# Attention with a feed-forward network: nine feed-forward passes of 512 tokens, fp32 scores for the first eight units, key sums over 1728 columns, and a fixed program order

## The chip, the cores and the metric

The kernel runs on one core of one Trainium2 chip. The metric is the device time of one execution in microseconds (us). Before the change three runs took 1312.46, 1313.7 and 1315.76 us; their median is 1313.7 us.

## The reference

Attention over 8 batches and 8 heads, 1152 keys and head size 64. Each two neighbouring queries are averaged first, so there are 576 query rows per head. The output of all heads, laid out as 4608 tokens of 512 numbers, goes through a feed-forward network with three input matrices and a maximum over their products.

```python
q_pool = q.reshape(B, H, S // factor, factor, D).mean(axis=3)
scores = scale * np.matmul(q_pool, k.transpose(0, 1, 3, 2))
scores = scores - np.max(scores, axis=-1, keepdims=True)
attn = np.exp(scores)
attn = attn / (np.sum(attn, axis=-1, keepdims=True) + 1e-09)
return np.matmul(attn, v).astype(np.float32)
...
h = np.maximum(np.maximum(x @ w1, x @ w2), x @ w3)
return (h @ w_out).astype(np.float32)
```

## The kernel before

**Units.** Two heads make a pair (32 pairs, four to a batch), and half of a pair's queries (288) make a unit `d` (64 units, eight to a batch). A unit holds all 1152 keys in nine steps of 128 keys on the partitions, with 2 x 288 columns for the two heads. Per step the TensorE makes the scores `pqk` (L596, L597), ACT copies them to `s` (L609) and DVE keeps a running maximum `acc` over the steps (L618). Then the maximum over the partitions is taken, DVE subtracts it (L743; for the second head of units 0 to 7 POOL does), ACT takes the exponential (L749), the TensorE multiplies with the values into `pav` (L790), and POOL adds the nine steps into `ksum` (L766, L768) for the denominator. In units 0 to 15 the TensorE adds all or part of the steps instead (`psum`, L874).

**Precision.** The scores and the feed-forward use the fp32r type, with every operand split into a high part and the rest. For keys and queries ACT casts the high part (L474, L481), POOL subtracts (L478, L485), and DMAs on the SP queue (`move_k`, `move_q`, L519) stack high and low parts on the 128 partitions in `kc` and `qq`; a score step is then two matmuls of 288 columns per head. `pav` and `psum` are plain fp32, and the two heads go to different columns of the array (`o.pav[64 * h : 64 * h + 64]`).

**Feed-forward.** Batch `b` is one pass of 576 tokens in two chunks of 288. A chunk of 128 hidden numbers is 12 matmuls (`ph`, L1127: four input slices times the products high-high, low-high, high-low); ACT copies the first of three products to `hm` (L1145), DVE takes the maximum with the other two (L1147), ACT and POOL split the result into `h` (L1155, L1158). The second layer is 18 matmuls per chunk and output slice (`po`, L1181), copied out by ACT (L1197) and stored. The weights, split once in pass 0, are read again in every later pass from `w_split` into a ring of two tiles. Pass `b` is put into the program beside the attention of batch `b + 1`; the last pass follows the attention.

**Order.** Every instruction belongs to a step with the steps it needs. `arrange` plays the program with costs (`pe`, `act`, `dve`, `pool`) and takes on each engine the ready step of lowest rank, from the numbers in `RANK` and `TUNE`. The order is fixed when the program is built; each engine then works its own list in order.

## Time and profile before

| | |
|---|---|
| median of three runs | 1313.7 us |
| span of the profiled execution | 1315.8 us |
| time of the profiled execution beside its span | 1315.8 us: the span is as long as the slowest of the three times (1315.76), so nothing lies around it |
| PE, POOL, DVE, ACT busy | 98%, 81%, 76%, 74% of the span |
| unit 8's first score copy | about 136 us |
| last score copy of unit 63 | 1193.3 us |
| read from and written to HBM | 158.47 MB, 22.02 MB |

A busy share says how much of the span has at least one instruction of the engine in it. Matmuls overlap in the records (one of 288 columns is shown with 296 ns, while they start some 132 ns apart), so what a matmul costs is read from how many start in a stretch, not from its length. Idle time stands behind the bar of a group, with the engine that ended it.

### The profile page before, as it was taken

To read this page: it belongs to the slowest core of one execution; us is meant where nothing else is said; L and a number is where in the kernel's file an instruction comes from. 1 tells how busy PE (TensorE), PEld (TensorE's weight loads), DVE (VectorE), ACT (ScalarE), POOL (GpSimd) and SP (SyncE) were. 2 spreads that over 40 slices of the span, in tenths; PEclk is the share of its full clock that TensorE was granted. 3 is DMA by queue.
4 is the path that set the end of the run, shared out by engine and by line. 5 is a ranking of instruction groups with operands and counts; after the bars stand their busy time and mean duration, and the time that the engine had idled before them with its cause. 6 is when DMAs were issued, how large, how long until landed. Compare 5 with 4: busy or idle time off the path is not lost.

```text
span 1315.8 us, 26773 instructions
## 1 busy us (share of the span) xinstructions
PE 1288.9 (98%) x9726; PEld 1112.9 (85%) x9726; DVE 998.9 (76%) x1602; ACT 972.7 (74%) x1863; POOL 1068.1 (81%) x894
## 2 busy tenths in 40 slices
PE   7899999999999999999999999999999999999999
PEld 6555788778888899888889988888899888888998
DVE  5687788988778878888888887888888877885120
ACT  6798788888777877778877887778777777775211
POOL 5678597989999998899988898999988999878210
PEclk7999999999999999999999999999999999999999
DMA  6766477877765676676766577666776567632544
GB/s 185 208 185 159 128 226 234 245 230 215 228 193 178 203 241 205 169 211 184 224 207 205 170 220 223 179 179 197 203 237 195 178 186 213 208 127 81 188 160 157
DMA packets 107795, 255.39 MB, mean 194 GB/s; under 512 B 14608, under 2 KB 78608, under 8 KB 98448
## 3 DMA queue, kind: packets, MB, share of 16 engines
q1 hardware_dynamic: 107376, 253.09, 63.8%
q8 instruction: 78, 1.28, 0.4%
q10 hardware_dynamic: 288, 0.59, 0.1%
q14 instruction: 53, 0.43, 0.1%
HBM read 158.47 MB, written 22.02 MB: 137 GB/s over the span
## 4 chain that ended last, share of the span: by engine, by line
PE 81%; DMA 7%; ACT 5%; POOL 3%; DVE 2%; issue 1%; SPq 1%; ACTq 0%; DVEq 0%; POOLq 0%
PE ph L1127 31%; PE pav L790 20%; PE pqk L596 10%; PE pqk L597 9%; PE po L1181 8%; DMA w<-w_split 3%; PE psum L874 2%; ACT s L609 2%; DMA qq<-qraw 2%; ACT s L749 1%; DMA kraw<-in_kT_dram 1%; DVE acc L618 1%; POOL ksum L768 1%; SPq L519 1%; DMA w<-in_win_dram 1%
## 5 line engine op out<-in xcount | busy, mean ns | idle before, releaser
L768 POOL TENSOR_TENSOR ksum<-ksum,s 128x576 f32<-128x576 f32 x360 | 517.9, 1442 | 9.9 <-ACT s L749 0.4
L1127 PE MATMUL ph<-xh,w 128*128 128x288 f32 x2304 | 511.7, 296 | 3.5 <-DMA w<-w_split 2.2
L609 ACT COPY s<-pqk 128x576 f32<-128x576 f32 x576 | 365.1, 639 | 103.7 <-PE pqk L597 97.5
L618 DVE TENSOR_TENSOR acc<-acc,pqk 128x576 f32<-128x576 f32 x448 | 333.7, 745 | 109.9 <-ACT s L609 106.1
L749 ACT ACTIVATE s<-s 128x864 f32<-128x864 f32 x384 | 351.6, 931 | 61.1 <-DVE s L743 58.1
L1127 PEld LDWEIGHTS ph<-xh,w 128*128 128x128 f32 x2304 | 387.7, 188 | 5.4 <-ACT hm L1145 2.2
L596 PE MATMUL pqk<-qq,kc 128*128 128x288 f32 x1152 | 336.1, 308 | 15.4 <-DVE acc L618 10.4
L1127 PE MATMUL ph<-xl,w 128*128 128x288 f32 x1152 | 339.5, 295 | 0.0
L597 PE MATMUL pqk<-qq,kc 128*128 128x288 f32 x1152 | 324.3, 298 | 0.0
L790 PE MATMUL pav<-s,v 128*64 128x288 f32 x2304 | 291.5, 408 | 0.0
L596 PEld LDWEIGHTS pqk<-qq,kc 128*128 128x128 f32 x1152 | 220.1, 191 | 56.7 <-DVE acc L618 20.5
L790 PEld LDWEIGHTS pav<-s,v 128*64 128x64 f32 x2304 | 160.5, 137 | 113.3 <-issue 9.1
L743 DVE TENSOR_TENSOR s<-s,spare 128x864 f32<-128x864 f32 x216 | 219.9, 1041 | 1.2
L597 PEld LDWEIGHTS pqk<-qq,kc 128*128 128x128 f32 x1152 | 220.8, 192 | 0.0
L1127 PEld LDWEIGHTS ph<-xl,w 128*128 128x128 f32 x1152 | 217.3, 189 | 0.0
L1181 PE MATMUL po<-h,w 128*128 128x288 f32 x1152 | 170.4, 295 | 2.3 <-ACT ob L1197 2.1
L1181 PEld LDWEIGHTS po<-h,w 128*128 128x128 f32 x1152 | 158.5, 188 | 3.9 <-ACT ob L1197 3.3
L743 DVE TENSOR_TENSOR s<-s,pmb 128x864 f32<-128x864 f32 x144 | 148.2, 1043 | 0.8
L1147 DVE TENSOR_TENSOR hm<-hm,ph 128x288 f32<-128x288 f32 x192 | 85.0, 443 | 71.5 <-PE ph L1127 71.0
L1158 POOL TENSOR_TENSOR h<-hm,h 128x288 fp32r<-128x288 f32 x96 | 76.9, 811 | 76.3 <-ACT h L1155 75.8
L766 POOL TENSOR_TENSOR ksum<-s 128x576 f32<-128x576 f32 x56 | 81.8, 1461 | 25.6 <-ACT s L749 25.0
L485 POOL TENSOR_TENSOR kraw<-kraw 128x1152 fp32r<-128x1152 f32 x31 | 83.2, 2684 | 19.3 <-ACT kraw L481 18.9
(62 smaller groups left out, 1035.0 us busy)
## 6 DMA issues: line engine op xcount, KB each, us to landing
w<-w_split SPq DMA_DIRECT2D x63, 1024.0 KB, 6.0
kc<-kraw SPq DMA_DIRECT2D x372, 96.0 KB, 3.5
qq<-qraw SPq DMA_DIRECT2D x248, 144.0 KB, 4.1
w<-w_split SPq DMA_DIRECT2D x28, 768.0 KB, 4.6
v<-in_vr_dram SPq DMA_DIRECT2D x32, 576.0 KB, 4.4
kraw<-in_kT_dram SPq DMA_DIRECT2D x31, 576.0 KB, 4.4
qraw<-in_qT_dram SPq DMA_DIRECT2D x31, 576.0 KB, 5.3
w<-in_win_dram SPq DMA_DIRECT2D x18, 512.0 KB, 4.8
```

The costliest lines, as they stand in the source:

```text
L485: vec[e].tensor_tensor(lo.bitcast(F32R), lo, o.hl[:, 0, x:y], op=ALU.subtract)
L596: nc.tensor.matmul(ps[:, h - hs[0], :QH], w, qq[:, 0, h], start=True, stop=False)
L597: nc.tensor.matmul(ps[:, h - hs[0], :QH], w, qq[:, 1, h], start=False, stop=True)
L609: nc.scalar.copy(o.s[kk // 3][:, kk % 3, slice(*hs)], o.ps[kk, hs][:, :, :QH])
L618: nc.vector.tensor_tensor(acc, acc, ps, op=ALU.max)
L743: vec[e].tensor_tensor(s, s, o.pb[h][:, None, :QH].broadcast_to([P, 3, QH]), op=ALU.subtract)
L749: nc.scalar.activation(s, s, AF.Exp, scale=SCALE)
L768: vec[e].tensor_tensor(o.ksum, o.ksum, x, op=ALU.add)
L790: nc.tensor.matmul(o.pav[64 * h : 64 * h + 64, :QH], pr.v[:, kk, h], o.s[kk // 3][:, kk % 3, h], start=(kk == 0), stop=(kk == NK - 1),)
L1127: nc.tensor.matmul(t.ps[:, :QH], w[:, a, kk], xx[:, kk, qs], start=(kk == 0 and i == 0), stop=(kk == 3 and i == 2),)
L1147: nc.vector.tensor_tensor(part[c], part[c], t.ps[:, :QH], op=ALU.max)
L1181: nc.tensor.matmul(t.ps[:, :QH], w[:, k : k + P], hh[:, kk, qs], start=(kk == 0 and i == 0), stop=(kk == 5 and i == 2),)
```

## The change

Five parts, in one diff.

- The feed-forward runs over `PASSES = [[512]] * 9`: nine passes with one chunk of 512 tokens. Pass boundaries no longer fall on batch boundaries, so a unit's output is split in up to two pieces (`pieces_of`), and the attention output lies in a ring of four halves (`RING`). The weights are fetched eight times instead of seven, into a ring of three tiles (`w3pool`). The second layer waits for each hidden slice alone, not for all.
- In units 0 to 7 (pairs 0 to 3, `WHOLE = 4`) the scores are one plain fp32 matmul per head and step, on the 64 partitions that the head's keys and queries have as loaded: head 0 on rows 0 to 63 of the array, head 1 on rows 64 to 127, each into a bank of its own. The casts, subtractions and stacking DMAs of these pairs go, and so do the inputs `fq` and `fk` laid out for pair 0.
- From unit 16 on POOL makes the key sums as two additions over three steps at once (1728 columns) and two of 576, instead of eight of 576.
- The order is a table, `ORDER`: one place for each step, in the order in which the code makes the steps. `arrange` sorts by it.
- The five groups of six warming matmuls are put among the first units' scores, where before all stood ahead of them.

```diff
-order = arrange(plan, {"ff": 2})
+ORDER = {
+    "warm": [1, 7, 37, 49, 67],
+    "table": [4],
+    "lead": [0, 6, 2, 3, 5],
...
+WHOLE = 4
+PASSES = [[512]] * 9
+START = [sum(map(sum, PASSES[:p])) for p in range(len(PASSES) + 1)]
+XW = max(map(sum, PASSES))
+RING = 4
...
+def arrange(plan):
+    place = {kind: iter(at) for kind, at in ORDER.items()}
+    for s in plan:
+        s.place = next(place[s.kind])
+    assert all(a.place < s.place for s in plan for a in s.after + s.pre)
+    return sorted(plan, key=lambda s: s.place)
...
+def mm(n):
+    return pe(3 * (n / 2.4 + 12.5))
...
                     for h in range(*hs):
-                        w = kc[:, h, kk % 3 * P : kk % 3 * P + P]
+                        if d < 2 * WHOLE:
+                            rows = slice(64 * h, 64 * h + 64)
+                            w, x = pr.k[rows, P * kk : P * kk + P], pr.q[rows, 1, QH * o.half : QH * o.half + QH]
+                            nc.tensor.matmul(ps[:, h - hs[0], :QH], w, x, start=True, stop=True)
+                            continue
+                        w, qq = pr.kc[kk // 3][:, h, kk % 3 * P : kk % 3 * P + P], pr.qq[o.half]
                         nc.tensor.matmul(ps[:, h - hs[0], :QH], w, qq[:, 0, h], start=True, stop=False)
                         nc.tensor.matmul(ps[:, h - hs[0], :QH], w, qq[:, 1, h], start=False, stop=True)
...
+        def thirds(e, i):
+            if i == 1:
+                room()
+                vec[e].tensor_tensor(o.three, o.s[0], o.s[1], op=ALU.add)
+            else:
+                vec[e].tensor_tensor(o.three, o.three, o.s[2], op=ALU.add)
+
+        def fold(e, i):
+            vec[e].tensor_tensor(o.ksum, o.ksum, o.three[:, i], op=ALU.add)
...
+    def pieces_of(b, half):
+        t = NQ * b + QH * half
+        for p, (x, y) in enumerate(zip(START, START[1:])):
+            lo, hi = max(t, x), min(t + QH, y)
+            if lo < hi:
+                yield p, lo - x, hi - lo, lo - t
...
+                wt[g] = (w3pool if place % 3 == 2 else wpool).tile([P, 2, 2, NPAIR, P], F32R, tag="w", name=f"w{b}_{g}")
...
                             for i, (a, xx) in enumerate(((0, xh), (0, xl), (1, xh))):
                                 nc.tensor.matmul(
-                                    t.ps[:, :QH],
+                                    t.ps[:, :n],
                                     w[:, a, kk],
                                     xx[:, kk, qs],
...
-                        "mm", at, n, [pe(396)], product, [tail[0]] + fetched[g] + (hdone if kk == 0 else []),
-                        take="ff" if kk == 0 else None, cols=864,
+                        "mm", at, done * NQ / total, [mm(n)], product, [tail[0]] + fetched[g] + hdone[kk, c],
+                        take="ff" if kk == 0 else None, cols=3 * n,
...
     finish[d - 1]([])
-    ffn(B - 1, [0, 1], d)
-
-    order = arrange(plan, {"ff": 2})
+    for p in range(B - 1, len(PASSES)):
+        ffn(p, d + 8 * (p - B + 1))
+
```

The first place is the ACT list at the program's start, before; names carry the unit (`s0` and `pqk0` are unit 0's), and `qq`, `kc` hold the split queries and keys.

```order
L372 DMA qraw0_0_120<-in_fq_dram 128x576 x2
L411 ACT_TABLE_LOAD
L411 COPY rest_117<-ones_99 128x1
L382 CAST qq0_0_149<-qraw0_0_120 128x288
L403 CAST kc0_0_164<-kraw0_129 128x384
L382 CAST qq0_0_149<-qraw0_0_120 128x288
L403 CAST kc0_0_164<-kraw0_129 128x384
L609 COPY s0_0_184<-pqk0_0_174 128x576
L609 COPY s0_0_184<-pqk0_1_179 128x576
L403 CAST kc0_1_192<-kraw0_129 128x768
L609 COPY s0_0_184<-pqk0_2_187 128x576
L403 CAST kc0_2_204<-kraw0_129 128x768
```

And the same list with the change.

```order
L242 DMA q0_122<-in_qT_dram 128x2x288
L223 ACT_TABLE_LOAD
L223 COPY rest_134<-ones_102 128x1
L460 COPY s0_0_151<-pqk0_0_145 128x576
L460 COPY s0_0_151<-pqk0_1_148 128x576
L460 COPY s0_0_151<-pqk0_2_154 128x576
L460 COPY s0_1_166<-pqk0_3_162 128x576
```

The six casts that stood ahead of and between unit 0's first score copies are gone; ACT's first work on data is the copy of a score step.

The second place is POOL around the key sums of unit 40, before; `xl`, `xr`, `kraw` and `ks` belong to other units and wait in the same list.

```order
L766 TENSOR_TENSOR ksum40_9274<-s40_0_8916 128x576
L949 TENSOR_TENSOR xl_114<-xr_112,xh_113 128x288
L833 TENSOR_TENSOR ks38_8991<-ks38_8991,ky39_64_9302 64x36
L768 TENSOR_TENSOR ksum40_9274<-ksum40_9274,s40_0_8916 128x576
L833 TENSOR_TENSOR ks38_8991<-ks38_8991,ky39_32_9316 32x36
L768 TENSOR_TENSOR ksum40_9274<-ksum40_9274,s40_1_8985 128x576
L949 TENSOR_TENSOR xl_114<-xr_112,xh_113 128x288
L768 TENSOR_TENSOR ksum40_9274<-ksum40_9274,s40_1_8985 128x576
L805 TENSOR_TENSOR xr_112<-xr_112,rs38_9386 128x288
L768 TENSOR_TENSOR ksum40_9274<-ksum40_9274,s40_1_8985 128x576
```

And with the change.

```order
L620 TENSOR_TENSOR ksum40_7613<-s40_0_7252,s40_1_7312 128x1728
L1071 TENSOR_TENSOR h3_6526<-hm3_5_0_7539,h3_6526 128x512
L622 TENSOR_TENSOR ksum40_7613<-ksum40_7613,s40_2_7360 128x1728
L715 TENSOR_TENSOR ks38_7595<-ks38_7595,ky39_64_7684 64x36
L625 TENSOR_TENSOR ksum40_7613<-ksum40_7613 128x576
L320 TENSOR_TENSOR kraw22_7642<-kraw22_7642 128x1152
L625 TENSOR_TENSOR ksum40_7613<-ksum40_7613 128x576
```

Eight additions have become four, and what stands between them (here a feed-forward half and a key preparation) now stands behind an addition of three times the columns.

The third place is PE where the attention ends and the feed-forward of the last tokens begins, before; `pav62` and `pav63` are the last two units' products with the values, `po6` the second layer of pass 6, `ph7` the first layer of pass 7.

```order
L790 MATMUL pav63_14832<-s63_2_14605,v31_14056 64x288 x6
L1181 MATMUL po6_0_0_14855<-h6_13591,w6_9_14722 128x288 x18
L1181 MATMUL po6_0_1_14878<-h6_13591,w6_9_14722 128x288 x18
L1181 MATMUL po6_1_0_14904<-h6_13591,w6_10_14799 128x288 x18
L1181 MATMUL po6_1_1_14935<-h6_13591,w6_10_14799 128x288 x18
L1181 MATMUL po6_2_0_14968<-h6_13591,w6_11_14908 128x288 x18
L1181 MATMUL po6_2_1_14994<-h6_13591,w6_11_14908 128x288 x18
L1181 MATMUL po6_3_0_15016<-h6_13591,w6_12_14963 128x288 x18
L1181 MATMUL po6_3_1_15040<-h6_13591,w6_12_14963 128x288 x18
L1127 MATMUL ph7_0_0_0_15065<-xh_113,w7_0_15020 128x288
```

And with the change.

```order
L1094 MATMUL po6_3_0_12053<-h6_10892,w6_12_11989 128x512 x18
L672 MATMUL pav62_12082<-s62_0_11586,v31_11517 64x288 x6
L672 MATMUL pav62_12082<-s62_1_11648,v31_11517 64x288 x6
L672 MATMUL pav62_12082<-s62_2_11702,v31_11517 64x288 x6
L672 MATMUL pav63_12125<-s63_0_11810,v31_11517 64x288 x6
L672 MATMUL pav63_12125<-s63_1_11846,v31_11517 64x288 x6
L672 MATMUL pav63_12125<-s63_2_11886,v31_11517 64x288 x6
L1029 MATMUL ph7_0_0_0_12163<-xh_115,w7_0_12029 128x512
```

Before, eight chunks of the second layer (18 matmuls of 288 columns each) stand between the last attention product and the first layer of pass 7, the last pass. With the change the whole second layer of pass 6 stands ahead of the last two attention products, pass 7 follows them at once, in matmuls of 512 columns, and pass 8 follows pass 7.

## Rows read from the trace of the kernel before

**Rows 1.** The page: busy time, share of the span and instructions of each engine.

```profile
PE 1288.9 (98%) x9726; PEld 1112.9 (85%) x9726; DVE 998.9 (76%) x1602; ACT 972.7 (74%) x1863; POOL 1068.1 (81%) x894
```

**Rows 2.** The page: the chain that ended last, by engine.

```profile
PE 81%; DMA 7%; ACT 5%; POOL 3%; DVE 2%; issue 1%; SPq 1%; ACTq 0%; DVEq 0%; POOLq 0%
```

**Rows 3.** Windows: start:end length, busy (instructions) by engine, granted clock, DMA.

```profile
0.00:9.00 9.00, 7.26 (x35) 7.09 (x36) 3.68 (x9) 3.17 (x6) 1.58 (x10) 1.00 0.58 199
9.00:136.00 127.00, 114.72 (x785) 71.85 (x784) 91.68 (x154) 102.89 (x179) 91.34 (x62) 0.89 0.65 182
...
283.00:1041.00 758.00, 753.96 (x5753) 669.71 (x5752) 627.65 (x984) 597.19 (x1159) 689.33 (x574) 1.00 0.68 202
...
1193.00:1237.00 44.00, 43.43 (x330) 39.17 (x330) 14.39 (x26) 16.83 (x41) 26.54 (x28) 1.00 0.43 150
1237.00:1316.00 79.00, 75.32 (x565) 74.81 (x564) 10.89 (x24) 13.18 (x32) 9.69 (x12) 1.00 0.44 160
```

**Rows 4.** Windows of the tiles ph and po alone, in the tail.

```profile
1241.00:1279.00 38.00, 37.64 (x284) 37.44 (x283) 6.81 (x15) 3.19 (x8) 1.00 0.46 167
...
1297.00:1310.00 13.00, 13.00 (x99) 12.92 (x98) 2.00 (x5) 1.00 0.54 190
```

**Rows 5.** A window at the half clock, and timeline of PE: start, us, instruction.

```profile
15.00:20.00 5.00, 4.30 (x16) 3.48 (x15) 2.43 (x4) 2.96 (x5) 2.25 (x2) 0.50 0.48 135
...
17.83 0.44 PE L597 MATMUL pqk<-qq,kc 128*128 128x288 f32 x1
18.07 0.44 PE L596 MATMUL pqk<-qq,kc 128*128 128x288 f32 x1
```

**Rows 6.** Timeline of weight loads and matmuls after a short idle.

```profile
8.62 0.19 PEld L596 LDWEIGHTS pqk<-qq,kc 128*128 128x128 f32 x1 [0.18 <-DVE kc L408]
8.72 0.19 PEld L597 LDWEIGHTS pqk<-qq,kc 128*128 128x128 f32 x1
...
8.62 0.40 PE L596 MATMUL pqk<-qq,kc 128*128 128x288 f32 x1
8.85 0.29 PE L597 MATMUL pqk<-qq,kc 128*128 128x288 f32 x1
```

**Rows 7.** Window of the tile pav; timeline of PE from pav to pqk.

```profile
500.00:1000.00 500.00, 116.36 (x936) 66.07 (x936) 10.24 (x26) 1.00 0.67 200
...
723.69 1.62 PE L790 MATMUL pav<-s,v 128*64 128x288 f32 x12
725.25 0.40 PE L596 MATMUL pqk<-qq,kc 128*128 128x288 f32 x1
```

**Rows 8.** Groups by line and form on POOL: count, busy us, mean ns, idle before.

```profile
L768 POOL TENSOR_TENSOR ksum<-ksum,s 128x576 f32<-128x576 f32 x360 | 517.9, 1442 | 9.9 <-ACT s L749 0.4
L485 POOL TENSOR_TENSOR kraw<-kraw 128x1152 fp32r<-128x1152 f32 x31 | 83.2, 2684 | 19.3 <-ACT kraw L481 18.9 <-DMA w<-w_split 0.2
L1158 POOL TENSOR_TENSOR h<-hm,h 128x288 fp32r<-128x288 f32 x96 | 76.9, 811 | 76.3 <-ACT h L1155 75.8
```

**Rows 9.** Groups by line and form on ACT: casts of keys and queries.

```profile
L481 ACT CAST kraw<-kraw 128x1152 fp32r<-128x1152 f32 x31 | 35.9, 1158 | 8.9 <-DMA kraw<-in_kT_dram 4.8 <-DMA qq<-qraw 4.0
L474 ACT CAST qraw<-qraw 128x576 fp32r<-128x576 f32 x31 | 20.9, 676 | 3.8 <-POOL qraw L471 2.7 <-DMA w<-w_split 0.5
```

**Rows 10.** Groups by line and form on DVE: maxima over scores and feed-forward.

```profile
L618 DVE TENSOR_TENSOR acc<-acc,pqk 128x576 f32<-128x576 f32 x448 | 333.7, 745 | 109.9 <-ACT s L609 106.1
L1147 DVE TENSOR_TENSOR hm<-hm,ph 128x288 f32<-128x288 f32 x192 | 85.0, 443 | 71.5 <-PE ph L1127 71.0
```

**Rows 11.** Timeline of ACT and POOL at the end of the attention.

```profile
1193.30 0.64 ACT L609 COPY s<-pqk 128x576 f32<-128x576 f32 x1 [1.08 <-PE pqk L597]
...
1225.49 0.80 POOL L949 TENSOR_TENSOR xl<-xr,xh 128x288 fp32r<-128x288 f32 x1 [0.55 <-ACT xh L946]
```

**Rows 12.** The page: DMA issues, KB each, us to landing; timeline: the last copy.

```profile
w<-w_split SPq DMA_DIRECT2D x63, 1024.0 KB, 6.0
...
1312.76 0.40 ACT L1197 COPY ob<-po 128x288 f32<-128x288 f32 x1 [1.99 <-PE po L1181]
```

More of the change, by code (lines that the diff above doesn't have):

```diff
@@ new lines, in loads @@
+        def loads(fn, parts, size, lead, eng, more):
+            if n:
+                gone = [qk[pairs[n - 2].last, NK - 1]] if n > 1 else pairs[0].kmoved + pairs[0].qmoved
+                return [step("load", r, [("sp", 0.5)], lambda e: fn(e, *parts[0]), gone + more, size=parts[0][1] * size)]
+            return [
+                Step(plan, "lead", [(eng if i == 0 else "sp", 0.4)], lambda e, x=x, y=y: fn(e, x, y), [], size=(y - x) * size)
+                for i, (x, y) in enumerate(parts)
+            ]
@@ new lines, in whole @@
+        o.qmoved = loads(load_q, qparts, 1, -1000, "act", [])
+        o.kmoved = loads(load_k, kparts, 0.5, -1001, "sp", o.qmoved)
+        inline("qq", o.qmoved)
+        inline("ksum", o.kmoved)
+        qs = [
+            step("prep", r + 0.01 * i, [(pool if n else dve)(y - x)], lambda e, x=x, y=y: qsum(e, x, y), [a])
+            for i, ((x, y), a) in enumerate(zip(qparts, o.qmoved))
+        ]
+        o.kready = {c: [o.kmoved[c % len(o.kmoved)]] for c in range(3)}
+        o.qready = {half: [qs[half % len(qs)]] for half in range(2)}
@@ L445, in load_v @@
+        loaded = o.kmoved + o.qmoved
+        if n == 1:
+            pairs[0].lv.after += loaded
+        o.lv = step(
+            "load",
+            r + 2,
+            [("sp", 0)],
+            lambda e: load_v(e, o, n, b, j),
+            [av[pairs[n - 2].last]] if n > 1 else loaded + ([pairs[0].lv] if n else []),
+            size=576,
+        )
+        inline("v", [o.lv])
     def load_v(e, o, n, b, j):
@@ L537, in heads @@
             o.qmoved += o.qready[half]
+            inline("qq", o.qready[half])
             if d == r:
                 for c in range(3):
-                    i = 3 * n + c - 4
-                    gone = qk[pairs[i // 3].last, 3 * (i % 3) + 2] if i >= 0 else None
+                    i = 3 * (n - WHOLE) + c - 4
+                    gone = qk[pairs[WHOLE + i // 3].last, 3 * (i % 3) + 2] if i >= 0 else None
                     o.kready[c] = [
@@ L764, in key @@
                 if kk == 1:
-                    o.ksum = small.tile([P, 2, QH], F32, tag="ksum", name=f"ksum{d}")
+                    room()
                     vec[e].tensor_tensor(o.ksum, o.s[0][:, 0], x, op=ALU.add)
@@ L967, in rest @@
                 for g in range(4):
-                    t = [step("psum", d, [("act", 0.3)], hand(g), t + [gone])]
+                    t = [step("psum", d, [("act", 0.3)], hand(g), t + [gone], pre=[spreads.get(15) if d == 17 else None])]
                 folded[d] = folded[d - 1] = t[0]
@@ L1143, in half @@
+                        if b == f == j == c == kk == 0:
+                            tail[0].pre += held
+                        done += 6 * n / QH / 2
+                    def half(e, t=t, j=j, c=c, f=f, n=n, part=part):
                         if j == 0:
-                            part[c] = small.tile([P, QH], F32, tag="hm", name=f"hm{b}_{f}_{c}", bufs=3)
-                            nc.scalar.copy(part[c], t.ps[:, :QH])
-                        else:
-                            nc.vector.tensor_tensor(part[c], part[c], t.ps[:, :QH], op=ALU.max)
@@ L1149, in ffn @@
-                    used = len(hm_read) + c - cs[0] - 3
+                            part[c] = small.tile([P, 512], F32, tag="hm", name=f"hm{b}_{f}_{c}", bufs=HM)
+                            nc.scalar.copy(part[c][:, :n], t.ps[:, :n])
+                        else:
+                            nc.vector.tensor_tensor(part[c][:, :n], part[c][:, :n], t.ps[:, :n], op=ALU.max)
+                    used = len(hm_read) + c - HM
                     first = [tail[0], prev[c] if j else hm_read[used] if used >= 0 else None]
-                    prev[c] = ffn_step("evac", at, n, [act(QH) if j == 0 else dve(QH)], half, first, give="ff")
+                    prev[c] = ffn_step("evac", at, done * NQ / total, [act(n) if j == 0 else dve(n)], half, first, give="ff")
```

540 lines of the change are left out of this document (191 added, 349 removed), and 6 rows, old and new, of tables (ORDER, TUNE).

## The prediction

> **What bounds the kernel now.** I read the busy shares first, then the chain that ended last, then the same shares stretch by stretch, since an average hides where the limits change. PE is busy for 98% of the span, the next engine (POOL) for 81% [rows 1], and PE holds 81% of the last chain [rows 2]. By stretches there are three regimes [rows 3]. From 9 to 136 us (units 0 to 7, no feed-forward to fill with) no engine is full: PE is busy for 114.7 of 127 us at a mean granted clock of 0.89, ACT for 102.9. From 283 to 1041 us PE is busy for 753.96 of 758 us, with POOL at 689.33, 91%. From 1193 us on PE works almost alone. So outside the first stretch a microsecond taken off PE's own work is a microsecond of the span, as long as POOL, the next, does not take over.
>
> PE's records overlap, so the price of a matmul is a pitch. In the tail 284 first-layer matmuls stand in 38.00 us (133.8 ns each) and 99 of the second layer in 13.00 us (131.3 ns) [rows 4]; I use 132.5 ns for 288 columns.
>
> **The feed-forward at 512 columns.** Before, a pass is 2 x (18 x 12 + 4 x 18) = 576 matmuls, and eight passes are 4608 x 132.5 ns = 610.6 us. After, a pass is 288 matmuls and nine are 2592. What one of 512 columns costs no row shows; the question is what the 132.5 ns are made of, because 288 columns at 2.4 GHz are only 120 ns.
> - At the half clock of 1.2 GHz (0.50 in the window) matmuls start 0.24 us apart [rows 5]: exactly 288 / 1.2 GHz and nothing else. So the 12.5 ns are not added to the columns at that clock; something about 130 ns long runs beside them, and shows only when the columns are shorter.
> - The weight load is such a thing. After a short idle the first load starts at 8.62, the second, which waits for the first to be taken over, at 8.72, and the second matmul at 8.85 [rows 6]: 0.10 for a load, then 0.13 to the next matmul, even with weights and columns free to overlap.
> - In fp32, where a record streams 288 columns in two cycles each (240 ns), 936 records are 116.36 us busy, 26 units of 4.475 us with 18 starts of two records each [rows 7]; less the last one's overhang that is 240 ns and at most a few more per start.
>
> So with 213.3 ns of columns the load should lie under them, and I take 215 ns: 2592 x 215 = 557.3 us, **53.3 us less**. The other ends: 12.5 ns on top of each matmul after all (225.8 ns, 585.3 us, 25.3 us less), or a cost in proportion to the columns (235.6 ns, 610.6 us, nothing less). Nothing below that: no row has a matmul that costs more per column with more columns.
>
> The Trainium skill's page "TensorE: Matmul & The Clock Gate", section "Back-to-back issue gap", gives a lone warm matmul N / 2.4 GHz plus 2.5 ns, 215.8 ns at 512 columns and 122.5 at 288. For 288 the rows have 132.5, so the measurement decides there; with the page's price on both sides the gain would be 4608 x 122.5 - 2592 x 215.8 ns = 5 us, with the measured price before it is 51. The 10 ns that the page does not have are what the first rival keeps.
>
> The copies and maxima of 512 columns replace two of 288: on DVE 443 ns for 288 and 745 for 576 [rows 10] give 0.68 us for 512 against 0.89, less on every engine, hidden as before. Weights: a tile serves 24 matmuls, 5.2 us, and lands in 6.0 [rows 12]; with three tiles its load has two tiles' time, 10.3 us, where it had 6.4. I cost it at nothing; if the cover went, it would be under 1 us per tile.
>
> **Scores of units 0 to 7.** 72 steps of four matmuls (0.53 us) become two fp32 matmuls on half the rows each. The nearest row is the pair in `pav`, on half the columns each: 4.475 / 9 = 0.50 us per pair [rows 7]. Beside each other: 2 us less in all; one after the other (2 x 0.48): 31 us more. I take them as beside each other, like `pav`, and at 0 for the span, since PE does not set the end in this stretch.
>
> The Trainium skill's page "TensorEngine Tiling (Array Packing)", section "Key Properties", speaks against it: a change of tiling mode drains the array. Twelve `pav` records take 1.56 us to the first score (723.69 to 725.25), where six starts at 4.475 / 18 = 0.249 are at most 1.49 [rows 7], so the drain is there and costs some 0.1 us. Some 70 such changes lie ahead of unit 8, about as many as before; were each to drain twice, PE would have 7 us more to do there.
>
> **The start.** Per pair ACT loses casts of 1158 and 676 ns [rows 9], POOL subtractions of 2684 ns and about 1.44 us [rows 8], for four pairs 7.3 and 16 us. ACT, the fullest engine after PE, goes from 102.9 to 95.6 us; if the stretch shrinks in proportion that is 9 us of 127. The first score waited for two casts and two subtractions in a row after its data (first place); at about half a microsecond each and a handover that is 3 us. **12 us less**, between 0 (another wait takes their place) and 20 (the stretches at half clock go too).
>
> **Key sums.** On POOL 576 columns take 1442 ns and 1152 take 2684 [rows 8], 2.156 ns per further column, so 1728 take 3.93 us. A unit's sums go from 8 x 1.442 = 11.5 to 2 x 3.93 + 2 x 1.44 = 10.7 us. Three times the small one (4.33) would make no gain; 3.73, with no fixed part, 1.2 us per unit. None of it is on PE's path; what matters is POOL's share. In 283 to 1041 us (40 units, five passes) POOL loses 40 x 0.8 = 32 us of sums and 10 of feed-forward halves (12 x 0.811 [rows 8] become 6 x 1.30 per pass), and gains 4 for units cut in two: 689 becomes 651. PE loses five passes of 76.3 - 61.9 us: 758 becomes 686. POOL's share goes from 91% to 95%, and each 3.93 us addition holds back what stands behind it (second place): the feed-forward's low half and with it the buffer `hm`, the key preparation, the next pass's input. I allow PE's idle time to grow from 0.5% to 2% of the attention, **14 us more**, with 2 and 45 as ends.
>
> **The end.** After the last score of unit 63, PE now has 18 + 72 matmuls of 512 columns (19.4 us) and two units of `pav` (9.0) before pass 7 (third place), 28.4 us. Before, 33 us passed from the last score's copy (1193.30) to the end of the first split that pass 7 needs (1226.3) [rows 11]; it was hidden behind pass 6. So PE waits some **4 us**, 0 to 8. The last copy starts 3.0 us before the end [rows 12] and is now of 512 columns, with a larger store: 0.5 us, together **5 us more**.
>
> **Sum.** -53.3 - 12 + 14 + 5 = -46 us on the profiled span of 1315.8, which equals the slowest of the three times, so nothing lies around it: 1269.5. The median of the runs is 2.1 us lower, so 1267.
>
> **Rivals.**
> - *The 12.5 ns stay on each matmul* (225.8 ns). For it: a cost per matmul at the full clock alone would also be invisible at half clock if it lies in a stage that the columns cover there. Against it: rows 6. 28 us more than the forecast, 6 fewer of idle time, since POOL then has 93%: 1289. Chance 0.22.
> - *The two heads' scores run one after the other.* For it: no row shows halves of the rows. Against: halves of the columns overlap [rows 7], and each head writes its own bank. 33 us more PE work against the forecast in a stretch where PE has a few us free: about 28, 1295. Chance 0.08.
> - *POOL takes over as the bound.* If its 69 us of idle in 758, waits for ACT and DVE, stay, the stretch takes 720 and not 696, for seven batches 34 us more: 1301. For it: 95%. Against: those waits are there because PE is slower. Chance 0.09.
> - *Slower than before: the long additions stall PE.* An addition holds POOL 2.5 us longer than one of 576. If what stands behind it is what PE waits for, PE loses 2.5 us each time; 96 of them are 240 us. From 20 of 96 on the gain is gone; at 24 or so the time is 1327. For it: POOL works in order, and POOL's results gate `h` and the input of the next pass. Against: PE's waits hardly name POOL before, 4 us idle in 758 [rows 3]. Chance 0.06.
> - The forecast itself, 1250 to 1285: 0.55.
>
> **Numbers.** The range 1246 to 1302 takes in the three rivals below 1302 and the start's better end, and leaves out two in ten. A measurement tells 0.3% (4 us) from no change. The forecast and the first three rivals are faster by more, 0.94; I move 0.03 of it to no change for costs that I have not named: faster 0.91, same 0.03, slower 0.06.
>
> **What would show it.** A stretch of the tail with `ph` alone: 215 ns per matmul (right) or 226 or 236. In `pqk0` to `pqk7`, the two heads' records a few ns apart and 0.5 us per step. POOL's 1728 columns at 3.9 us, and its share between 92% and 96% in the middle with PE's idle under 3%. Unit 8's first score copy at about 124 us. A PE gap of about 4 us before pass 7, and 2 x 62 us from there to the end. The prediction is wrong if the middle shows PE waiting for POOL or for `hm`, or if 512 columns cost over 226 ns.

## The result, and the profile after

The changed kernel takes 1297.2 us (median of four runs, 1295.3 to 1297.7) against 1314.0 for the kernel before on the same chip, a ratio of 0.987, 95% interval [0.985, 0.988]. That is 17 us less where the prediction had 46; the profiled spans stand at 1295.6 and 1315.8, 20.2 apart. So the direction was right, the size was not.

The page of the changed kernel, busy time by engine and the chain by engine; they answer to [rows 1] and [rows 2].

```profile
PE 1271.2 (98%) x7710; PEld 962.7 (74%) x7710; DVE 992.7 (77%) x1513; ACT 941.9 (73%) x1770; POOL 1014.5 (78%) x683
...
PE 85%; ACT 5%; DVE 4%; DMA 3%; issue 2%; SPq 1%; POOL 0%; DVEq 0%; ACTq 0%; POOLq 0%
```

PE is still busy for 98%, with 2000 matmuls fewer, and POOL has left the chain. Stretch by stretch (start:end length, busy and count by engine in the order PE, weight loads, DVE, ACT, POOL, then clock, DMA share, GB/s), to be held against [rows 3]: the start up to unit 8, the middle, and all after the last score.

```profile
6.00:111.00 105.00, 99.16 (x774) 49.59 (x770) 87.47 (x145) 93.52 (x164) 70.93 (x49) 1.00 0.41 135
...
259.00:986.00 727.00, 720.76 (x4359) 565.44 (x4356) 621.73 (x923) 576.16 (x1094) 645.93 (x402) 1.00 0.73 216
1129.00:1295.00 166.00, 162.79 (x737) 129.51 (x735) 30.41 (x48) 37.75 (x83) 50.13 (x51) 1.00 0.51 181
```

The start has lost its stretches at half clock (1.00 where [rows 3] has 0.89). The middle has POOL at 89%, less than the 91% before, not the 95% expected: POOL's busy time came as worked out (645.93 us for 651), but the stretch has 727 us and not 686. And the pitch, first and second layer alone in the tail (windows of the tiles ph and po; the first two columns after the length are PE and weight loads), against [rows 4]:

```profile
1158.07:1208.55 50.48, 50.48 (x216) 40.49 (x216) 7.57 (x11) 3.53 (x6) 1.00 0.46 162
1224.89:1275.28 50.39, 50.39 (x216) 40.38 (x215) 7.56 (x11) 3.53 (x6) 1.00 0.54 189
...
1208.56:1224.88 16.32, 16.32 (x72) 13.33 (x71) 1.76 (x3) 1.00 0.74 253
```

216 matmuls of 512 columns in 50.4 us are 233.3 ns each in the first layer, 72 in 16.32 are 226.7 in the second. The prediction had 215. Two things stand in these rows: 512 columns cost almost as much per column as 288, and the two layers differ by 6.6 ns with the same columns, type and clock. The first made the loss; the second became a faster kernel (e3).

POOL's and DVE's groups by line and form (count, busy us, mean ns, idle before), which answer to [rows 8] and [rows 10]:

```profile
L622 POOL TENSOR_TENSOR ksum<-ksum,s 128x1728 f32<-128x1728 f32 x48 | 188.4, 3925 | 7.3 <-ACT s L601 6.5
L625 POOL TENSOR_TENSOR ksum<-ksum 128x576 f32<-128x576 f32 x96 | 137.6, 1433 | 3.5
...
L1058 DVE TENSOR_TENSOR hm<-hm,ph 128x512 f32<-128x512 f32 x108 | 73.1, 677 | 106.1 <-PE ph L1029 105.5
L1071 POOL TENSOR_TENSOR h<-hm,h 128x512 fp32r<-128x512 f32 x54 | 70.3, 1307 | 85.2 <-ACT h L1068 85.2
```

Here each size came as worked out: 3.93 us for 1728 columns, 0.68 for a maximum of 512, 1.31 (1.30) for the low half.

### The profile page after: what moved, and what is told of

It reads as the page before. It is cut to its first block, busy times and chain, and to the rows that moved or that the text cites. A ratio compares the mean times of both kernels' runs of the same rounds, so it can differ in the third digit from the quotient of the medians.

```text
span 1295.6 us, 22055 instructions
## 1 busy us (share of the span) xinstructions
PE 1271.2 (98%) x7710; PEld 962.7 (74%) x7710; DVE 992.7 (77%) x1513; ACT 941.9 (73%) x1770; POOL 1014.5 (78%) x683
## 4 chain that ended last, share of the span: by engine, by line
PE 85%; ACT 5%; DVE 4%; DMA 3%; issue 2%; SPq 1%; POOL 0%; DVEq 0%; ACTq 0%; POOLq 0%
PE ph L1029 33%; PE pav L672 20%; PE pqk L447 10%; PE po L1094 10%; PE pqk L448 9%; DVE acc L469 3%; ACT s L460 2%; PE pqk L444 2%; ACT s L601 1%; PE psum L756 1%; DMA w<-in_win_dram 1%; DVE s L595 1%; DMA kraw<-in_kT_dram 1%; DMA qq<-qraw 1%; SPq L346 1%
## 5 line engine op out<-in xcount | busy, mean ns | idle before, releaser
L1029 PE MATMUL ph<-xh,w 128*128 128x512 f32 x1296 | 453.0, 396 | 0.3 <-DVE hm L1058 0.3
L447 PE MATMUL pqk<-qq,kc 128*128 128x288 f32 x1008 | 290.1, 305 | 12.1 <-DVE acc L469 8.8
L448 PE MATMUL pqk<-qq,kc 128*128 128x288 f32 x1008 | 280.8, 296 | 0.0
L1029 PEld LDWEIGHTS ph<-xh,w 128*128 128x128 f32 x1296 | 244.0, 188 | 48.3 <-POOL qraw L306 0.5
L1029 PE MATMUL ph<-xl,w 128*128 128x512 f32 x648 | 256.8, 396 | 0.0
L620 POOL TENSOR_TENSOR ksum<-s,s 128x1728 f32<-128x1728 f32 x48 | 187.8, 3913 | 20.3 <-ACT s L601 17.4
L622 POOL TENSOR_TENSOR ksum<-ksum,s 128x1728 f32<-128x1728 f32 x48 | 188.4, 3925 | 7.3 <-ACT s L601 6.5
L1094 PE MATMUL po<-h,w 128*128 128x512 f32 x648 | 162.3, 391 | 0.0
L1058 DVE TENSOR_TENSOR hm<-hm,ph 128x512 f32<-128x512 f32 x108 | 73.1, 677 | 106.1 <-PE ph L1029 105.5
L625 POOL TENSOR_TENSOR ksum<-ksum 128x576 f32<-128x576 f32 x96 | 137.6, 1433 | 3.5
L1029 PEld LDWEIGHTS ph<-xl,w 128*128 128x128 f32 x648 | 122.0, 188 | 16.9
```

The source lines that it names most:

```text
L447: nc.tensor.matmul(ps[:, h - hs[0], :QH], w, qq[:, 0, h], start=True, stop=False)
L448: nc.tensor.matmul(ps[:, h - hs[0], :QH], w, qq[:, 1, h], start=False, stop=True)
L620: vec[e].tensor_tensor(o.three, o.s[0], o.s[1], op=ALU.add)
L622: vec[e].tensor_tensor(o.three, o.three, o.s[2], op=ALU.add)
L625: vec[e].tensor_tensor(o.ksum, o.ksum, o.three[:, i], op=ALU.add)
L1029: nc.tensor.matmul(t.ps[:, :n], w[:, a, kk], xx[:, kk, qs], start=(kk == 0 and i == 0), stop=(kk == 3 and i == 2),)
```

## Experiments

Every time is a median beside the kernel before; "changed" is the kernel of the diff, 1297.2. Theories A, B and C are those of the expectation that stands ahead of each result.

**e1, the pitch alone.** TensorE with nothing else to do, row by row of 36 matmuls of one form.

```python
for i in range(count):      # per: 12 or 18 matmuls to a PSUM tile, as in ph and po
    ...
    a, x = pairs[i % len(pairs)]
    nc.tensor.matmul(
        ps[:, :n], a, x, start=(i % per == 0) or change, stop=(i % per == per - 1) or change
    )
```

> This kernel computes none of the reference: it holds rows of 36 matmuls, one row for each form, and writes filler to the output. TensorE starts are read row by row. Rows: fp32r with 64 to 512 columns in the operand layout of the second feed-forward layer (polike, cols) and of the first (phlike, phcols); the two layouts crossed; one weight tile for all; one moving operand for all; each matmul a start of its own; zeros in place of data; bf16 (half) and fp32 (full); with VectorE or with loads running beside. Theory A, the step of the prediction (a weight load of about 130 ns runs beside the columns): 64 to 288 columns all near 130 ns, 512 at 215. Theory B, the prediction's first rival (a fixed addition of about 12.5 ns to each matmul): 128 columns 66 ns, 256 119, 288 132.5, 384 172.5, 512 226, and bf16 the same or less. Theory C, a price per column (0.425 to 0.449 ns instead of 0.417) with a smaller fixed part: 128 columns 61 to 64 ns, 256 118, 384 173 to 176, 512 227 to 233. For the 6 ns between the first layer (233 in the changed kernel) and the second (227): if the layout of the operands makes them, phlike shows 233 and polike 227, and the crossed rows say which operand; if the data make them, zeros are nearer 213 and the two layouts agree; if the work beside makes them (VectorE's reading of PSUM, loads), both show 227 alone and the rows with VectorE or loads show 233.

Windows of e1, one for each form (PE has the 36 of the form, and a few cut by the edges; an fp32 matmul counts as two): phlike and polike, with operands laid out as in the first and the second layer, at 512 columns; operands whose rows are shifted by 32 bytes each; zero weights; 256, 288, 384 columns; bf16 with 512.

```profile
38.86:47.02 8.16, 8.16 (x38) 6.76 (x36) 0.00 (x0) 0.00 (x0) 0.00 (x0) 1.00 0.01 2
47.02:55.18 8.16, 8.16 (x38) 6.76 (x36) 0.00 (x0) 0.00 (x0) 0.00 (x0) 1.00 0.00 0
79.66:88.03 8.37, 8.37 (x38) 6.76 (x37) 0.00 (x0) 0.00 (x0) 0.00 (x0) 1.00 0.00 0
...
130.80:139.19 8.39, 8.39 (x37) 6.76 (x36) 0.00 (x0) 0.00 (x0) 0.00 (x0) 1.00 0.00 0
...
166.13:170.47 4.34, 4.34 (x39) 4.34 (x37) 0.00 (x0) 0.00 (x0) 0.00 (x0) 1.00 0.00 0
170.47:175.21 4.74, 4.74 (x38) 4.74 (x37) 0.00 (x0) 0.00 (x0) 0.00 (x0) 1.00 0.01 3
180.49:186.74 6.25, 6.25 (x39) 6.25 (x38) 0.00 (x0) 0.00 (x0) 0.00 (x0) 1.00 0.00 0
...
223.71:231.46 7.75, 7.70 (x37) 3.62 (x36) 0.00 (x0) 0.00 (x0) 0.00 (x0) 1.00 0.00 0
```

From start to start: fp32r takes 120 ns at 256 columns, 132 at 288, 173 at 384, 226.7 at 512; bf16 takes 215.8 at 512 and 122.5 at 288, fp32 242.5 at 288 for each of a matmul's two records. Theory A falls: 256 columns run at 120 ns, so nothing 130 ns long lies beside them. Theory B, the first rival, holds at 256, 320, 384 and 512: columns / 2.4 GHz plus 13.3 ns; 288 has 11.8, 448 and 480 have 17 to 20. bf16 and fp32 have 2.5 (fp32 on two cycles a column in each record). Data and company don't matter: zeros in both operands, VectorE beside and loads at 391 GB/s beside all leave 226.7 to 228. And phlike has 226.7 here, not 233; but three rows have 232.5 to 233.3: rows 32 bytes apart, zero weights with real data, real weights with zero data. What these three share is where weights and operand lie in their partitions: 128 against 256 bytes modulo 512, or shifting by 32; the fast rows of 512 columns have the same remainder in both. In the changed kernel the inputs lie at 448, the weights and the hidden tile at 480.

**e2, the distance.**

```python
o = off // 4      # off: bytes away from likeness; row is 512 in the long rows
return [(w[:, i % 12, :m], g[:, o + row * i : o + row * i + n]) for i in range(12)]
```

> This kernel computes none of the reference: rows of 36 fp32r matmuls again, filler as output. In e1 the same 512 columns took 226.7 ns where weights and moving operand lay alike in their partitions modulo 512 bytes (128 and 128, 256 and 256), and 232.5 to 233.4 where they did not (256 and 128, 128 and 256, rows 32 bytes apart). Rows long: 512 columns with the moving operand 0 to 1040 bytes away from that likeness. Rows short: the same for 288 columns. Rows fewer: 96, 64 and 32 weight columns. Theory A (distance modulo 512 decides): 226.7 at 0 and at 1024 bytes, 229 to 237 at the others, all with one mean of about 233 or in steps with the distance. Theory B (the three slow rows of e1 have another cause, such as the tile itself): all long rows at 226.7. For the fixed part of 13.4 ns: if it is the reading of the weights beside the stream, it goes with their columns, so 64 weight columns 220 ns and 32 columns 217; if it belongs to the matmul, 226.7 in all three.

Windows of e2 with the operand 0, 16, 32, 64, 256 and 496 bytes away from likeness, all with 512 columns:

```profile
42.39:50.55 8.16, 8.16 (x37) 6.76 (x36) 0.00 (x0) 0.00 (x0) 1.00 0.00 0
50.55:58.89 8.34, 8.34 (x37) 6.77 (x36) 0.00 (x0) 0.00 (x0) 1.00 0.00 0
58.89:67.30 8.41, 8.41 (x38) 6.75 (x37) 0.00 (x0) 0.00 (x0) 1.00 0.00 0
75.69:83.94 8.25, 8.25 (x37) 6.76 (x36) 0.00 (x0) 0.00 (x0) 1.00 0.00 0
109.15:117.33 8.18, 8.18 (x38) 6.76 (x37) 0.00 (x0) 0.00 (x0) 1.00 0.00 0
150.75:158.91 8.16, 8.16 (x37) 6.76 (x36) 0.00 (x0) 0.00 (x0) 1.00 0.01 2
```

Theory A, in steps with the distance: 226.7 at 0, 231.5 at 16, 233.4 at 32, 229.2 at 64, 227.2 at 256, 226.9 at 496, 227.8 at 1024, and 229 to 234 at the others. The rows at 256, 496 and 1024 settle at 226.7 after their first one to nine matmuls. That it goes modulo 512 rests on 1024 and 1040, which repeat 0 and 16; as 256 is as fast as 0, a period of 256 is not ruled out. With 288 columns it is 131.6 to 133.5 throughout, so the kernel before could hardly show it. The fixed 13 ns are not the reading of the weights: 96, 64 or 32 weight columns take 230 to 232. What they are stays open.

**e3, the placement in the kernel.**

```diff
     xl = cpool.tile([P, NPAIR, XW], F32R, name="xl")
+    cpool.tile([P, 120], F32, name="gap")
```

> The changed kernel with 480 bytes per partition left free behind the two input tiles, so that inputs, weights and hidden tile lie alike modulo 512 bytes (all 448; in the changed kernel inputs 448, weights and hidden 480). Nothing else is changed, the order neither. Theory A (the distance between weights and input makes the first layer's 233 ns): ph 226.7 ns, po stays at 227, 1944 x 6.6 ns = 12.8 us less than the changed kernel's 1297: 1284. Theory B (something else in the first layer, and the distance is chance): ph 233 and 1297. Theory C (ph 227, but what waits behind it eats the gain): 1288 to 1297 with more idle time of TensorE.

The 480 bytes move everything that is allocated behind them, so that inputs, weights and hidden tile all lie at 448. 1288.3 us, ratio to before 0.981 [0.979, 0.984], 9 us less than the changed kernel, and the fastest kernel of this study. First and second layer in its last pass:

```profile
1220.73:1269.69 48.96, 48.96 (x216) 40.35 (x215) 7.56 (x11) 3.52 (x6) 1.00 0.55 195
...
1269.69:1285.70 16.01, 16.01 (x71) 13.28 (x71) 1.76 (x3) 1.00 0.40 148
```

226.7 ns from start to start in both (the second window ends just ahead of the 72nd start): theory A, in the tail to the tenth. In the attention the first layer has 230.5 (233.2 before the shift), since other matmuls cut it into runs of 3 to 18, most of 3 or 6: there the starts are 230 to 232 ns apart in the first five matmuls of a run and 226.7 from the twelfth on. So the feed-forward, from start to start with waits, is 6.7 us shorter than in the changed kernel and not 12.8; the profiled spans differ by 5.7 (1289.9 and 1295.6), the medians by 9.

**e9, the scores' rows too (on top of e3).**

```diff
-qpool.tile([P, 2, 2, QH], F32R, tag="qq", ...)
+qpool.tile([P, 2, 2, KC], F32R, tag="qq", ...)[:, :, :, :QH]
```

> e3 with the four rows of each query tile 1536 bytes apart instead of 1152 (96 columns of each row unused), so that the moving operand of every score matmul of the units from 8 on also lies like its weights modulo 512 bytes. In e3 the first layer has 227 ns in the tail but 230 in the attention, where scores stand between its matmuls. Theory A (the scores' likeness is what is missing): ph and po nearer 227 in the attention, scores at 131.7 ns instead of 133, 1500 x 3 ns + 2016 x 1 ns = 6 us less than e3's 1288: 1282. Theory B (each change between the two kinds of matmul costs by itself): as e3 within 2 us.

1291.5, ratio 0.983 [0.981, 0.985], which overlaps with e3's; the first layer in the attention stays at 230.4 ns. So the scores' likeness is not what is missing. Theory B, that the change between kinds of matmul costs by itself, fits this and the starts in e3's runs; no run isolates it.

**e11, 512 columns issued as 256 twice.**

```diff
-nc.tensor.matmul(t.ps[:, :n], w[:, a, kk], xx[:, kk, qs], ...)
+for z in (0, n // 2):
+    nc.tensor.matmul(t.ps[:, z : z + n // 2], w[:, a, kk], xx[:, kk, lo + z : lo + z + n // 2], ...)
```

> The changed kernel with each feed-forward matmul of 512 columns issued as two of 256 with the same weights, in the same place: the width is undone for TensorE alone, while copies, sums, loads, passes and order stay. By e1 256 columns take 119.8 ns in a row, so 239.6 for two against 233.4 in the first layer and 231 to 227 in the second. Theory A (every nanosecond of pitch is one of the span): 1944 x 6.3 + 648 x 9 = 18 us, 1315. Theory B (the 512 columns gave nothing to the span, something else sets the middle): 1297 to 1302. Theory C (one is longer than e1 has it, because weights of 128 columns come twice as often beside the other engines' work): over 1325.

The first layer of the pass before the last:

```profile
1165.01:1216.23 51.22, 51.22 (x432) 51.17 (x432) 7.57 (x11) 3.52 (x6) 1.00 0.46 160
```

118.6 ns each, a little better than e1's 119.8, 120 in the second layer. From start to start, waits included, all feed-forward matmuls add up to 621.2 us, 10.4 more than the changed kernel's 610.8, and the time is 1307.8, 10.6 more. So theory A with a smaller size, since the halves of the first layer run at 118.6 and not at 119.8: a nanosecond of pitch is a nanosecond of the span, and 512 columns against two of 256 are worth 10 us.

**e4, the key sums narrow, in the places of the wide ones.** The wide sums begin with unit 16, not with unit 8 as the expectations of e4 and e8 have it.

```diff
-vec[e].tensor_tensor(o.three, o.s[0], o.s[1], op=ALU.add)
...
+vec[e].tensor_tensor(o.ksum, o.s[0][:, 0], o.s[0][:, 1], op=ALU.add)
+for kk in range(2, 6) if i == 1 else range(6, NK):
+    vec[e].tensor_tensor(o.ksum, o.ksum, o.s[kk // 3][:, kk % 3], op=ALU.add)
```

> The changed kernel with the key sums of the units from 8 on taken back to eight additions of 576 columns, five of them in the place of the first addition of 1728, three in the place of the second, none in that of the two folds; the order is otherwise the same. Theory A (the prediction's term: POOL's work is off the path, only its share counts): POOL gets 11.5 us for a unit's sums where it had 10.7, 30 to 40 us more in 727, from 89% to about 93%; time within 4 us of 1297. Theory B (the long additions cost idle time of TensorE, the 14 us of the prediction): 1285 to 1293. Theory C (the wide sums made the room that TensorE's 99% needs): over 1303, with TensorE waiting for POOL's results.

1353.2, ratio 1.030 [1.028, 1.033]: theory C by the time. PE's waits in 259 to 1035 us (total, times, longest):

```profile
PE pqk L447 <- DVE acc L469: 15.8, 17, 1.9
PE po L1094 <- POOL h L1071: 5.1, 3, 2.6
PE pqk L447 <- DVE acc L466: 4.6, 3, 2.7
PE ph L1029 <- POOL xl L836: 3.0, 1, 3.0
```

PE now waits for POOL's low halves, which in the changed kernel it never does there. More of its waits name DVE's maximum, and DVE and ACT in turn wait for POOL's small steps: ACT for 41.6 us (`ks` and `qraw`) where it was 5.9, DVE for 18.7 (`ks` and `xr`) where it was nothing. But this edit does two things: more POOL work (1050.2 us in all for 1014.5), and some 7.2 us of it (five additions of 1.43) at a stretch.

**e10, the same amount in small pieces.**

```diff
+vec[e].tensor_tensor(idle, idle, idle, op=ALU.mult)    # behind each of the four additions
```

> The changed kernel with one tiny product on POOL (16 columns of an idle tile, about 0.2 us) behind each of the four key additions of a unit from 16 on, so 0.8 us more of POOL per unit, as eight additions of 576 columns would cost, but with the results in their old places. In e4 the same amount came with a first addition of 7.2 us instead of 3.9 and cost 56 us; in e6 and e8 the width was worth 6.6 us to the narrow side under another order. Theory A (POOL has room: 89% of the middle, and e4's loss is that of the place): 1297 to 1303. Theory B (POOL's work is what TensorE waits for in this order): 48 x 0.8 = 38 us, 1325 to 1340.

1302.1, 5 us more, with POOL at 667.05 us in 259 to 986 (645.93) and at 1044.7 in all, nearly as much as in e4. Theory A: POOL's amount is nearly free; what e4 lost beyond that comes from its long stretches.

**e6, e7, e8, the parts under the old scheduler.** `arrange` of the kernel before, with its ranks, makes the order of the new steps.

```diff
-for s in arrange(plan):
-    s.fn(s.engine)
+for _, s, e in arrange(plan, {"ff": 2}):
+    s.fn(e)
...
-PASSES = [[512]] * 9        # e7 only
+PASSES = [[288, 288]] * 8
...
-RING = 4                    # e7 only
+RING = 2
...
-for kk in range(1, o.mix if o.mix < NK else 0):      # e8 only: eight key steps of 576 columns
+for kk in range(1, o.mix):
```

> The changed kernel with all its parts, but the order made by the list scheduler of the kernel before (its ranks, lags and clock model) instead of the table. Theory A (the table is worth little, the parts make the gain): 1297 to 1305. Theory B (the parts need the table: the long additions and the passes that cut units in two leave TensorE waiting in an order made for other steps): 1310 to 1345, with the middle's idle time at 3 to 6% where it is 0.9% now.

> As e6, with the feed-forward taken back to eight passes of two pieces of 288 columns (and the ring of attention outputs cut to the two halves that such passes need). Against e6 this is the width alone. Theory A (the pitches measured in the traces: 4608 x 132.5 = 610.6 us against 1944 x 233.3 + 648 x 228 = 601.3): 9 us slower than e6, less if this order waits elsewhere. Theory B (the prediction: 215 ns): 53 us slower. Theory C (passes of whole batches suit this scheduler better, since no unit is cut in two): as fast as e6 or faster.

> As e6, with the key sums of the units from 8 on as eight steps of 576 columns, which the scheduler places one by one as in the kernel before. Against e6 this is the width of the key sums alone, without the forced places of e4. Theory A (the prediction: long additions cost idle time of TensorE): 5 to 14 us faster than e6. Theory B (POOL's work counts, 0.8 us for a unit): 0 to 10 us slower. Theory C (e4's 56 us are the price of the additions themselves): over 30 us slower.

e6 takes 1398.6 (ratio 1.065), e7 1337.6 (1.018), e8 1392.1 (1.060). All three sets of parts are slower than before under this order, whose ranks were found for other steps. e6 goes beyond its theory B. In e7 against e6 theory C holds and more: eight passes of whole batches are 61 us faster there. That units cut in two make the difference is not shown, as e7 also fetches the weights once less. PE waits for DVE's maximum for 50.7 us in e6 and for 21.9 in e7, and the mean granted clock is 0.962 and 0.990; the two together are not worked out to the 61 us. e8 is 6.6 us faster than e6: theory A by its size, but a small part of e6's loss. So the table of places is worth 101 us to these parts, and nothing here says what the old scheduler would reach with new ranks.

**e5 and e12, the removed load of the start put back.** Three casts and three subtractions of 576 columns per pair, in front of the first scores (e5; pair 0's in pieces of 288), or sixteen of each, two with each of the units 0 to 7 (e12).

```diff
+nc.scalar.copy(xr[:, 3, NQ:].bitcast(F32R), xr[:, 2, NQ:])
+nc.gpsimd.tensor_tensor(xr[:, 1, NQ:], xr[:, 2, NQ:], xr[:, 3, NQ:], op=ALU.subtract)
```

> The changed kernel with the removed load put back at the start, on idle memory and with no one waiting for its results: for each of the first four pairs three casts of 576 columns on ACT (2.0 us; the kernel before had 1.8) and three subtractions of 576 on POOL (4.3 us; 4.1 before). The scores stay in fp32. Theory A (the prediction: ACT's share sets this stretch): the first score copy of unit 8 goes from 111.3 to 119 to 121, the time up by about as much, 1305. Theory B (the stretches at half clock are most of the start's gain, and they return when TensorE has more pauses): 125 to 136 and a granted clock under 0.95 there, 1311 to 1320. Theory C (neither: fewer steps in a row between load and score, and the order): 111 to 114, within 4 us of 1297.

> As e5, the removed load put back (16 casts of 576 columns on ACT, 16 subtractions on POOL, e5 had 15 of each), but spread over units 0 to 7, two with each unit's subtractions on POOL, not in front of the pairs' first scores. Theory A (ACT's and POOL's share set the stretch): unit 8's first copy at 111.3 + 10 = 121. Theory B (pauses of TensorE before the first scores, and the half clock behind them, made e5's 22.7 us): 111 to 116, granted clock 1.00. Theory C (any added work here falls on the path): 130 or more.

Unit 8's first copy came at 134.0 and 133.2 us, the times were 1318.9 and 1324.3. That looked like theory B of e5 (granted clock 0.56 from 20 to 30 us, 0.50 from 70 to 80) and C of e12, but ACT's waits in the first 134 us say that the edits added waits of their own, which the kernel before doesn't have: a cast waits for the subtraction that reads the last one's result (e5), an exponential waits behind POOL's added work (e12). Neither run tells the theories apart.

```profile
ACT xr L250 <- POOL xr L251: 14.1, 11, 1.5
```

That is e5 (total, times, longest), and this is e12:

```profile
ACT s L605 <- POOL s L599: 10.9, 12, 1.4
```

**e13, e14, e15, the load without those waits.** e13 is e5 with a subtraction that doesn't read the cast; e14 has ACT's casts alone, spread; e15 POOL's subtractions alone, spread and behind the unit's own.

```diff
-xr[:, 2, NQ : NQ + m], xr[:, 3, NQ : NQ + m], op=ALU.subtract
+xr[:, 2, NQ : NQ + m], xr[:, 2, NQ : NQ + m], op=ALU.subtract
```

> As e5 (three casts of 576 columns on ACT and three subtractions of 576 on POOL in front of the first scores of each of the first four pairs, results unused), but the subtractions no longer read what the casts write, so that neither engine waits for the other. Theory A (ACT's share, 9.8 us of added casts): unit 8's first copy at 119 to 122. Theory B (pauses ahead of the first scores and the half clock behind them): 122 to 136, clock under 0.95 in some stretch. Theory C (e5's 22.7 us were the added wait): 111 to 115.

> The changed kernel with ACT's part of the removed load alone, 16 casts of 576 columns (0.65 us each, 10.4 us), two per unit over units 0 to 7, on idle memory. Theory A (ACT's share sets the stretch one to one): unit 8's first copy 10 us later, 121 to 122. Theory B (ACT has gaps that take them): 111 to 115.

> The changed kernel with POOL's part alone, 16 subtractions of 576 columns (1.44 us each, 23 us), each behind one of the unit's own subtractions. Theory A (POOL has gaps in the start, about 70% busy there): unit 8's first copy at 111 to 115. Theory B (POOL's own results for the exponentials come late and the stretch grows with it): 118 to 130.

Unit 8's first copy on ACT (start, us, instruction), in the changed kernel:

```profile
111.32 0.64 ACT L460 COPY s<-pqk 128x576 f32<-128x576 f32 x1 [0.30 <-PE pqk L448]
```

The same copy in e13:

```profile
117.81 0.64 ACT L467 COPY s<-pqk 128x576 f32<-128x576 f32 x1 [0.30 <-PE pqk L455]
```

The traces give less added work than the expectations: pair 0's pieces in e13 have 288 columns, two of the sixteen pieces of e14 and of e15 come behind this copy, and a subtraction that reads one tile twice took 1.15 us, not 1.44. So the copy comes 6.5 us later for 8.7 us of casts in e13 (beside 14.4 of subtractions), 6.4 later for 9.5 of casts in e14 (117.7), and 9.0 later for 16.1 us of POOL in e15 (120.3); the times are 1304.5, 1303.8 and 1305.3. ACT's and POOL's amounts each come through in part, at 56 to 75%: e13 and e14 lie between theory A and the theory of gaps, e15 in B. Both together in front (e13, with a clock of 0.83 from 10 to 20 us) cost no more than either alone and spread.

## Why the prediction was wrong, step by step

**The feed-forward at 512 columns (-53.3 us; measured about -8.6).** This is the step that failed. 1944 x 233.2 + 504 x 230.1 (second layer in the attention) + 144 x 226.8 ns (in the tail) = 602.0 us, against the 610.6 of before; from start to start, waits included, it is 610.8 against 618.8. The working took [rows 5] and [rows 6] for a weight load that hides under long columns. e1 shows no such thing: 256 columns run at 120 ns. The 12.5 ns of the kernel before are there on fp32r matmuls of every width from 256 columns up, 11.8 to 20 ns and at 512 columns 13.3, and [rows 5] says only that they are absent at half clock. [Rows 6] was over-read: a delay after an idle time is no price in a running stream. The first rival had the mechanism (225.8 ns for 226.7 measured in the second layer). The 6.6 ns that even it lacked in the first layer are the placement, shown by e2 and by e3's tail; in the attention the placement gives back 2.7 of them. With the placement mended the time is 1288 beside that rival's 1289, though not by the same sum, as other terms moved too. The bound "nothing less" was the end nearest to what came.

The Trainium skill's page "TensorE: Matmul & The Clock Gate", section "Back-to-back issue gap", which the prediction set against its price, gives a lone warm matmul N / 2.4 GHz plus 2.5 ns. e1, where matmuls follow each other, agrees for bf16, with 122.5 and 215.8, and for fp32 with two cycles a column, 242.5. It doesn't for fp32r, which is what this kernel runs. The 10 ns that the prediction could not place belong to the type.

**The start (-12; measured -24.5).** Unit 8's first copy went from 135.82 to 111.32 us. The range's better end named the half clock, and that went: 0.89 to 1.00. But the reason, ACT's share, was only part: e13 puts about the removed load back (ACT 8.7 us, where 8.6 less of casts stand ahead of that copy than before) and loses 6.5. With the same new parts and the old scheduler (e6, e7) unit 8 comes at 134.1 and 131.1, 2 to 5 us earlier than before. The window of e6 from 20 to 40 us has the half clock again (the clock is the third number from the end):

```profile
20.00:40.00 20.00, 17.48 (x96) 7.05 (x94) 16.18 (x26) 18.14 (x33) 15.92 (x12) 0.67 0.38 135
```

So most of the gain needs the order of the table, which the prediction didn't price at all: with these parts the table is worth 22.7 us of the start against the old order (134.1 to 111.3).

**Scores of units 0 to 7 (0).** Right that the two heads lie beside each other: the eight records of two steps take 1.17 us from their first start to the next tile's, where one after the other, at 242.5 ns (e1), they would take 1.9.

```profile
60.76 1.24 PE L444 MATMUL pqk<-q,k 64*128 64x288 f32 x8
61.93 0.69 PE L756 MATMUL psum<-s,ones 128*32 128x288 f32 x8
```

That is 0.59 us a step for the 0.50 of the prediction. The starts of two pairs that are 236 ns apart within a kind are 333 to 340 apart around each change of kind, 0.1 us more. The pqk records of units 0 to 7 take 42 us from start to start where they took 55 (a distance over 0.3 us counted as 0.3), partly because no half clock falls on them now. What that is worth to the span no run shows apart from the order.

**Key sums and idle time (+14; measured +14, elsewhere).** Taking each start-to-start distance of score and feed-forward matmuls in the attention beyond 131.8, 233.3 and 227 ns (132 for the feed-forward before), PE lost 23 us before and 37 after. The size is right by luck, as the reason is wrong: the increase lies in units 8 to 23 (10 before, 24 after), mostly between two scores, and PE waits there for DVE's maximum (7.8 us of named waits for 3.0 before). From unit 24 on, where the wide additions are as well, it is 13 us in both. POOL fell to 89%, and e10 shows that 0.8 us more per unit would have cost 5. The increase in units 8 to 23 has no experiment of its own, and its cause stays open.

**The end (+5; measured 0.7).** The last values and pass 7 follow without the gap of 4 us:

```profile
1154.81 3.32 PE L672 MATMUL pav<-s,v 128*64 128x288 f32 x26
1158.07 0.50 PE L1029 MATMUL ph<-xh,w 128*128 128x512 f32 x1
```

The last copy and its store came as worked out: the copy starts at 1291.83 us, 3.8 us before the end, where it was 3.0.

**The sum.** -8.6 - 24.5 + 14 + 0.7 = -18.4 us of the 20.2 between the profiled spans; 1.8 are not assigned. The feed-forward brought 45 us less than forecast; the start and the end, 17 us better together, are why 1297 still lies in the range of 1246 to 1302, and the working priced only half of the start's part.

**The rivals.** "The 12.5 ns stay" was the right one. The two heads one after the other, and POOL as the bound, did not come. "The long additions stall PE" did not come in this order, though e4 shows that long stretches on POOL can do it: 56 us, there for 7.2 us at a stretch.

## What to carry to other kernels

A price per matmul is measured at the size and in the type that the change brings, before it is multiplied by thousands: one row of 36 in a loop would have told 215 from 227. Where a stream is bound by TensorE, look at where weights and moving operand lie modulo 512 bytes; here it was 3% of a layer for a gap of 480 bytes. An order belongs to the steps that it was made for: lengthening steps under a fixed order can cost far more than their work (e4), and so can giving new steps the old order's ranks (e6).

## What the runs showed of the hardware that was not expected

- fp32r at the full clock: 13.3 ns on top of the columns at 256, 320, 384 and 512, 17 to 20 at 448 and 480, against 2.5 in bf16 and fp32 (e1).
- The pitch at 512 columns goes from 226.7 to 233.6 with the distance of weights and moving operand modulo 512 bytes (e2; 0 and 256 settle alike); at 288 it stays within 131.6 to 133.5. After another kind of matmul it takes about ten matmuls to settle at 226.7 (e3; in e1, ten behind the shifted rows).
- 128 columns in fp32r took 213 ns each in e1, with the granted clock at 0.50, which is twice 128 / 1.2 GHz. The rows of 64 to 192 columns have mean granted clocks of 0.79, 0.50 and 0.67 and are not compared with the others.

```profile
152.54:160.26 7.72, 7.72 (x38) 7.72 (x38) 0.00 (x0) 0.00 (x0) 0.00 (x0) 0.50 0.01 2
```
